# A third of a batch spread over two experts, small copies moved to ScalarE, and the first pair's sums moved into the third expert

## The chip, the core and the metric

The kernel runs on one NeuronCore of one Trainium2 chip. The metric is the device time of one execution in microseconds (us); lower is better. Shown are the median of 3 runs and one further execution that was profiled. The engines are TensorE (PE, with PEld for its weight loads), VectorE (DVE), ScalarE (ACT), GpSimd (POOL) and SyncE (SP), which here only issues DMAs.

## What is computed

Three stages follow one another. The input has 4 batches of 3072 rows of 256 values (12288 tokens).

```python
X = rfft(x, axis=1)                          # spectral layer, per batch
Yr = Xr @ w_r - Xi @ w_i + b_r ; Yi = Xr @ w_i + Xi @ w_r + b_i
Y = soft_threshold(Yr, 0.01) + 1j * soft_threshold(Yi, 0.01)
x = irfft(Y)                                 # rows go on as tokens
...
e = argmax(x @ w_gate)                       # 8 experts, 384 places each, first come first served
h = relu(disp @ w1[e]) ; y = h @ w2[e]       # 256 -> 1024 -> 256
out = gate * y                               # 0 for tokens without a place
...
h = out @ w_in ; g = h * sigmoid(h)          # 256 -> 2048 -> 256
return g @ w_out
```

An expert has 384 places, so no more than 3072 tokens get past the second stage. With this input the first batch and the first third (1024 rows) of the second fill all places, and the rest of the input is not transformed: that branch of the program (`far`, and `experts` with `again`) does not run.

## The kernel before, in words

Every matmul of the experts and of the last stage is done in three products (`mm3`, lines 206 to 210): each float32 operand is split into a rounded high part and a low remainder (`split`, lines 202 to 204: the high part by `hi`, L192, on ACT; the low part by `lo`, L200, on DVE or POOL), and PE multiplies high by high, low by high and high by low.

**Spectral part.** `near` transforms batch 0 and batch 1 up to about 190 us. The spectrum of batch 1, multiplied and thresholded, is stored by `kphase` to the DRAM tensor `b_d` (L497, on ACT's queue). What is left of batch 1, its last inverse step for the first 1024 rows, is `third` (lines 569 to 626). It has four pieces n = 0 to 3. For each, `rows(n)` fetches two blocks of 96 x 1024 values from `b_d` (384 KB each, L587, tile `br`, or `bi` and `by` where the block lies in memory lent by the tiles `ms` and `yT`), multiplies them (L590), copies the result out of PSUM (L595, ACT) and stores the tokens in four DMAs (L597). `gate(n)` transposes the tokens (L604), copies them out (L606, DVE, tile `aT`), multiplies by the gate's weights (L612), and for every second piece makes the choice of an expert (`choose`). Then `route` gives the 1024 tokens their places and `slots` makes the index lists of experts 3 to 7.

**Experts.** `experts` (lines 949 to 1038) goes through phases 0, 1, 2, E, 3, 4, E+1, 5, 6, E+2, 7, E+3: eight experts (`first_ffn`), and between them four parts of the last stage, each for a pair of experts (`second_ffn`). An expert's rows are gathered by indirect DMA (`gather`, L1084, tile `xg`), scaled by the gate (`turn`, L1095, DVE, three tiles of 128x256), transposed and split. Its loop has nine steps (lines 1113 to 1127): step j makes block j of the hidden layer (6 matmuls, tile `hp`), evicts it (L1120 ACT, L1121 DVE, tiles `hh` and `hl`) and adds block j-1 to the output (6 matmuls, tile `y`). The output has two halves, copied to `yf` (L1130 by ACT, L1131 by DVE). A counter n counts the steps over all phases: n = 1 to 9 is expert 0, 10 to 18 expert 1, 19 to 27 expert 2.

The weights of an expert come in four quarters of two loads of 256 KB (L1066, tile `st`, four buffers), each cast to a high part by ACT (L192, tile `w`) and completed by DVE or POOL. For experts 0 and 1 they are asked for one quarter at a time in the steps of expert 0 (`lazy`, line 1002). They are read from float32 arrays; the last stage's weights are 64-bit floats that DVE narrows (lines 880 to 901).

**Pairs.** `pair` (lines 1133 to 1164) turns the two outputs of a pair into the seven split operands of a product scheme with seven products in place of eight: four sums or differences by DVE (L1151, L1154, L1156, L1159), each split (tiles `yT` and `ms`). For the first pair it is called when phase E begins, and its first and last instruction are ordered behind `self.made`, the one-hot comparison of `route` (L756, tile `pm`).

**What sets the order.** A generator `beside` (lines 969 to 981) holds the rest of batch 1; `experts` advances it when the counter n reaches the value it last yielded. It yields 7, then 8, 10, 12, 14 and 16: `rows(0)` is written at n = 7, `rows(1)` and `gate(0)` at 8, `rows(2)` and `gate(1)` at 10, `rows(3)` and `gate(2)` at 12, `gate(3)` at 14, and `route`, `slots` and the rest at 16. The program is not run in the order in which it is written: the framework (`schedule_with_timeline_sim=True`) plays a timeline of its own and fixes each engine's order by it. `after(a, b)` tells it to put `a` behind `b` without a semaphore. In `rows` only the first matmul is put behind `self.lasty`, the newest `y` matmul; the fetches are not. Each engine and each DMA-issuing queue then runs its instructions strictly in that order.

Of the kernel before, what the change touches and what calls it, by code (L numbers as in the profile page):

```python
# [9 lines left out]
F32 = mybir.dt.float32  # L10
FR = mybir.dt.float32r
I32 = mybir.dt.int32
ALU = mybir.AluOpType
# [6 lines left out]
Q = 96  # L20
# [3 lines left out]
P = 128  # L24
# [16 lines left out]
RING = 2  # L41
LATE = 3
PACE = {4: 2, 5: 5, **{n: GT - 1 for n in range(6, 12)}}
HOLD = {10: "lt", 14: "bs", 18: "tb"}
BIG = 65536.0
UP = 65536.0
# [109 lines left out]
class Kernel:  # L156
# [412 lines left out]
    def third(self, b, res):  # L569

        nc, bp, ps, wg, CH = self.nc, self.bp, self.ps, self.wg, self.CH
        v = nc.vector
        c4 = self.c4[:Q, 64:]
        bv = self.bds[b].rearrange("k (r u g) c -> (k r) u (g c)", r=4, u=4)
        od = self.attn[0][b * S:b * S + QB * TW].rearrange("(q u g) d -> u q (g d)", u=4, g=GT)
        res[b] = self.chosen(1)
        idle = self.mg.tile([P, 3, 2, CH], F32, tag="ms", name="bi", bufs=1)
        room = {n + 2: idle[:Q, n] for n in range(3)}
        room[5] = self.mh.tile([P, 2, CH], F32, tag="yT", name="by", bufs=1)[:Q]

        def rows(n):
            pt = ps.tile([P, CH], F32, tag="ps", name="ps2")
            for w in range(2):
                br = room.get(2 * n + w)
                if br is None:
                    br = bp.tile([Q, 2, CH], F32, tag="xt", name="br", bufs=self.sb)
                nc.sync.dma_start(out=br, in_=bv[:, 2 * w:2 * w + 2, n * CH:(n + 1) * CH])  # L587
                for z in range(2):
                    u = 2 * w + z
                    ins = nc.tensor.matmul(pt[u * QB:(u + 1) * QB], c4, br[:, z], start=True, stop=True).ins  # L590
                    if b == 1 and not u:
                        self.after(ins, self.lasty)
            ao = bp.tile([P, 2, 2, P], F32, tag="ao", name="ao2")
            aof = ao.rearrange("p g h d -> p (g h d)")
            nc.scalar.copy(aof, pt)  # L595
            for u in range(4):
                nc.sync.dma_start(out=od[u, :, n * CH:(n + 1) * CH], in_=aof[u * QB:(u + 1) * QB])  # L597
            return ao

        def gate(n, ao):  # L600
            tp = ps.tile([P, 2, 2, P], F32, tag="ps", name="tp")
            for g in range(2):
                for h in range(2):
                    nc.tensor.transpose(tp[:, g, h], ao[:, g, h], self.ident)  # L604
            aT = bp.tile([P, 2, 2, P], F32, tag="aT", name="aT", bufs=1)
            v.tensor_copy(aT, tp)  # L606
            if n % 2 == 0:
                self.lg = ps.tile([P, P], F32, tag="ps", name="lg")
            for h in range(2):
                for g in range(2):  # L610
                    at = COL * (2 * (n % 2) + g)
                    nc.tensor.matmul(self.lg[at:at + COL], wg[:, h], aT[:, g, h], start=h == 0, stop=h == 1)  # L612
            if n % 2:
                ls = bp.tile([P, P], F32, tag="ls", name="ls", bufs=1)
                nc.scalar.copy(ls, self.lg)
                lt = ps.tile([P, 4, COL], F32, tag="ps", name="lt")
                nc.tensor.transpose(lt.rearrange("p g e -> p (g e)"), ls, self.ident)
                self.choose(lt.rearrange("p (o g) e -> p o g e", o=1)[:, :, :, :E], res[b], slice(2 * n - 2, 2 * n + 2))

        ao = {}  # L620
        for n in range(GT // 2 + 1):
            if n < GT // 2:
                ao[n] = rows(n)
            if n:
                gate(n - 1, ao.pop(n - 1))
            yield

    def is2(self, b, qbs, res):
# [320 lines left out]
    def experts(self, again=False):  # L949
        tc = self.tc  # L950
        tag = "b" if again else "a"
        st = self.ex

        def pool(name, bufs=1, **kw):
            return st.enter_context(tc.tile_pool(name=name + tag, bufs=bufs, reuse_waits="tile", **kw))

        right = dict(side="right")
        ps = dict(space=bass.MemoryType.PSUM)
        self.mq, self.mx, self.mh = pool("mq", 3, **right), pool("mx", 2, **right), pool("mh", 2, **right)
        self.ph, self.pm = pool("ph", 3, **right, **ps), pool("pm", 2, **right, **ps)  # L960
        self.again = again
        self.wo = pool("mo").tile([P, 2, DFF // P, D], FR, name="wo")
        self.mg, self.mc = pool("mg", 2), pool("mc")
        self.zr = self.mc.tile([P, 2 * D], FR, name="zr")

        def zeros():
            self.nc.gpsimd.tensor_copy(self.zr[:, D:], self.zt[:, 0])

        def beside():

            with self.stream("b", 2, "left"):
                yield 7
                for n, _ in enumerate(self.third(1, self.res)):
                    yield 8 + 2 * n
                tiny = self.mc.tile([P, 1], F32, name="tiny")
                self.route(1, (0,), self.res)
                self.sl.extend(self.slots(self.mc, EARLY, E, self.sel, "t")[0])
                self.after(self.nc.scalar.activation(tiny, self.zt[:, 0, :1], AF.Silu).ins, self.exps)
                self.filled()
                zeros()  # L980
            self.po, self.mb = pool("po", **ps), pool("mb")

        fw = self.ffn_out()
        if again:
            self.raws = self.out_rows()
            zeros()
            self.sl = self.compact(self.mc)
            self.po, self.mb = pool("po", **ps), pool("mb")
            side = iter(())
            for _ in self.ffn_in(0, 8):  # L990
                pass
        else:
            self.sl = list(self.early)
            side = beside()
        order = [0, 1, 2, E]
        for q in range(3, E, 2):
            order += [*range(q, min(q + 2, E)), E + q // 2]
        xs, self.ys, self.unit = {}, {}, {}
        xg = {e: self.gather(e) for e in order[:2]}
        xs[0] = self.turn(xg.pop(0))  # L1000
        ws = {e: self.weights(e, n) for e, n in zip(order[:2], (3, 4))}
        lazy = {0: (0, 1), 2: (0, 2), 3: (1, 0), 4: (0, 3), 5: (1, 1), 6: (1, 2), 7: (1, 3)}
        due = next(side, None)
        n = 0
        for at, ph in enumerate(order):
            if ph == E:
                for _ in side:
                    pass
                pre = self.pair(None if again else self.made)
            part = self.first_ffn(ph, xs.pop(ph), ws[ph][0]) if ph < E else self.second_ffn(ph - E, pre)  # L1010
            if ph >= E:
                next(part)
            after = order[at + 1] if at + 1 < len(order) else E
            if after < E and after not in ws:
                xg[after] = self.gather(after)
                ws[after] = self.weights(after, 4 if ph == E else 0)
            for m, _ in enumerate(part):
                n += 1
                if not at and m in lazy:
                    e, z = lazy[m]  # L1020
                    ws[e][1](z, self.rectified)
                while due is not None and due <= n:
                    due = next(side, None)
                if n in LOADS:
                    next(self.raws, None)
                if n in AHEAD or (ph == E and m < 2):
                    next(fw, None)
                if ph >= E:
                    if ph == E and 3 <= m < 7:
                        ws[after][1](m - 3, self.evicted)  # L1030
                    for _ in range(2):
                        self.zero_out()
                if m == 5:
                    behind = self.evicted
                if m == 6 and after < E:
                    xs[after] = self.turn(xg.pop(after), behind)
            if ph < E and ph > 1 and ph % 2:
                pre = self.pair()
# [53 lines left out]
    def turn(self, rows, behind=None):  # L1092
        xg, gw = rows
        for j in range(SC):
            ins = self.nc.vector.tensor_scalar(xg[:, j], xg[:, j], gw[:, j:j + 1], None, ALU.mult)  # L1095
            if behind:
                self.after(ins.ins, behind)
        xT = self.mx.tile([P, 2, 2, CAP], FR, tag="xT", name="xT")
# [7 lines left out]
    def first_ffn(self, e, xT, ws):  # L1106
# [21 lines left out]
            yield  # L1128
        y = self.ys[e] = self.mg.tile([P, 2, CAP], F32, tag="yf", name="yf", bufs=3)
        nc.scalar.copy(y[:, 0], yp[0])  # L1130
        nc.vector.tensor_copy(y[:, 1], yp[1])  # L1131

    def pair(self, behind=None):

# [256 lines left out]
```

## Time and profile before

| | |
|---|---|
| median of 3 runs | 616.54 us (615.39 to 617.16) |
| the profiled execution, its own time | 617.55 us |
| its span, from the first to the last instruction | 615.8 us |
| mean granted TensorE clock over the span | 0.988 |
| busy: PE / DVE / ACT / POOL | 593.4 / 424.7 / 339.3 / 187.0 us |

The span has three stretches: up to about 180 us the spectral part, from there to about 266 us the experts 0 to 2 with the rest of batch 1 and the start of phase E, and then the alternating phases up to 607 us, with the last scattered stores behind them. A row of the waits names the instruction that waited, what released it, the total, the count and the longest. A row of a timeline has the start, the duration, engine, line, operation, output and inputs, shape, count, and in brackets the idle time before it and its releaser. A clock of 1.00 is 2.4 GHz and 0.50 is 1.2 GHz.

### The profile page before, as it was taken

Reading aid. Unit: us, or ns where it says so; the run is one execution under the profiler, and the core shown is the slowest. Engines: PE = TensorE matmul, PEld = TensorE weight load, DVE = VectorE, ACT = ScalarE, POOL = GpSimd, SP = SyncE. Lnnn points to the kernel's source line nnn. Section 1 sums busy time; section 2 is a strip of 40 time slices with the busy share of each in tenths; the row PEclk is TensorE's granted clock in tenths of the full one; section 3 lists DMA queues with packets and bytes.
Section 4 is the critical chain, followed back from the end, with each engine's and each line's share of the span. In section 5 each row is a group of like instructions: output and inputs, shape, how many; then the busy total and the mean of one; then the engine's idle time right before and its main releaser. Section 6 shows DMA issues by size and latency. Waiting matters only on the chain. (4 is left out here: it accounts for less than half of the span.)

```text
span 615.8 us, 11426 instructions
## 1 busy us (share of the span) xinstructions
PE 593.4 (96%) x4104; PEld 556.1 (90%) x4104; DVE 424.7 (69%) x844; ACT 339.3 (55%) x723; POOL 187.0 (30%) x189
## 2 busy tenths in 40 slices
PE   9999999999989799899999999999999999999994
PEld 9887799667988589789999999999999999989994
DVE  2468765449977589998876786587587577486563
ACT  2546554336525465556765756655567556365562
POOL 1001110002053023177453505435403442154433
PEclk9999999999999799989999999999999999999998
DMA  8829775996357976433633532404433230010001
GB/s 223 254 78 277 249 219 168 250 278 180 105 183 209 248 226 191 143 120 99 197 120 116 169 125 97 155 23 138 150 113 106 91 100 26 0 65 27 16 2 56
DMA packets 65755, 86.09 MB, mean 140 GB/s; under 512 B 5812, under 2 KB 55608, under 8 KB 65688
## 3 DMA queue, kind: packets, MB, share of 16 engines
q1 hardware_dynamic: 53720, 69.53, 37.8%
q10 hardware_dynamic: 9664, 9.44, 5.2%
q0 software_dynamic: 2304, 6.29, 3.2%
q8 instruction: 34, 0.56, 0.4%
q14 instruction: 33, 0.27, 0.2%
HBM read 54.31 MB, written 30.93 MB: 138 GB/s over the span
## 5 line engine op out<-in xcount | busy, mean ns | idle before, releaser
L1289 DVE TENSOR_TENSOR u<-h,u 128x384 f32<-128x384 f32 x224 | 117.9, 552 | 59.9 <-PE h L210 51.6
L1199 ACT ACTIVATE u<-u 128x384 f32<-128x384 f32 x128 | 64.6, 522 | 73.1 <-DVE u L1289 71.1
L209 PE MATMUL o<-wo,gl 128*128 128x256 f32 x354 | 94.5, 280 | 0.9 <-DVE gl L200 0.9
L210 PE MATMUL o<-wo,gh 128*128 128x256 f32 x354 | 94.6, 280 | 0.0
L208 PE MATMUL o<-wo,gh 128*128 128x256 f32 x354 | 83.1, 280 | 0.0
L200 POOL TENSOR_TENSOR ring<-mt,ring 128x384 fp32r<-128x384 f32 x32 | 38.0, 1190 | 136.3 <-ACT ring L192 136.3
L200 POOL TENSOR_TENSOR gl<-u,gh 128x384 fp32r<-128x384 f32 x62 | 64.8, 1060 | 29.6 <-ACT gh L192 29.5
L209 PEld LDWEIGHTS o<-wo,gl 128*128 128x128 f32 x354 | 66.5, 188 | 1.2 <-DVE gl L200 1.2
L210 PEld LDWEIGHTS o<-wo,gh 128*128 128x128 f32 x354 | 66.5, 188 | 0.0
L192 ACT CAST gh<-u 128x384 fp32r<-128x384 f32 x126 | 63.1, 509 | 5.7 <-PE o L210 4.0
L208 PEld LDWEIGHTS o<-wo,gh 128*128 128x128 f32 x354 | 62.4, 188 | 0.0
L208 PE MATMUL yp<-wri,xk 128*128 128x256 f32 x188 | 56.1, 298 | 0.0
L210 PE MATMUL yp<-wri,xk 128*128 128x256 f32 x188 | 54.0, 287 | 0.0
L209 PE MATMUL yp<-wri,xk 128*128 128x256 f32 x188 | 53.7, 286 | 0.0
L192 ACT CAST w<-st 128x512 fp32r<-128x512 f32 x64 | 38.6, 619 | 23.5 <-DMA st<-in_moe_w 15.7
L200 DVE TENSOR_TENSOR w<-st,w 128x512 fp32r<-128x512 f32 x56 | 39.6, 717 | 17.1 <-ACT w L192 12.0
L1120 ACT ACTIVATE hh<-hp 128x384 fp32r<-128x384 f32 x64 | 31.1, 489 | 35.4 <-PE y L209 13.7
L1121 DVE SCALAR_TENSOR_TENSOR hl<-hp,hh 128x384 fp32r<-128x384 f32 x64 | 34.9, 552 | 21.6 <-ACT hh L1120 16.3
L200 POOL TENSOR_TENSOR wi<-na,wi 128x256 fp32r<-128x256 f32 (+1 forms) x8 | 8.1, 1012 | 132.9 <-ACT wi L192 132.9
L208 PE MATMUL hp<-xT,w 128*128 128x384 f32 x128 | 43.8, 343 | 4.2 <-ACT w L192 4.1
L200 DVE TENSOR_TENSOR gl<-u,gh 128x384 fp32r<-128x384 f32 x64 | 42.8, 669 | 2.2 <-ACT gh L192 2.1
L208 PE MATMUL y<-hh,w 128*128 128x384 f32 x128 | 43.7, 341 | 0.5 <-ACT hh L1120 0.5
(254 smaller groups left out, 1543.1 us busy)
## 6 DMA issues: line engine op xcount, KB each, us to landing
st<-in_moe_w SPq DMA_DIRECT2D x64, 256.0 KB, 2.9
out<-zt SPq DMA_DIRECT2D x48, 256.0 KB, 3.5
b_d<-bo ACTq DMA_DIRECT2D x12, 512.0 KB, 3.1
mt<-mixed SPq DMA_DIRECT2D x32, 192.0 KB, 2.3
xt<-in_x SPq DMA_DIRECT2D x15, 384.0 KB, 6.7
nt<-in_moe_w_in SPq DMA_DIRECT2D x8, 512.0 KB
nt<-in_moe_w_out SPq DMA_DIRECT2D x16, 256.0 KB, 3.0
a_d<-ao SPq DMA_DIRECT2D x8, 384.0 KB, 3.4
```

Source lines behind the costliest of these rows:

```text
L192: self.lastact = self.nc.scalar.copy(dst, src)
L200: return e.tensor_tensor(dst, src, raw(hi), ALU.subtract).ins
L208: first = nc.tensor.matmul(out, lh, rh, start=start, stop=False)
L209: nc.tensor.matmul(out, ll, rh, start=False, stop=False)
L210: return first.ins, nc.tensor.matmul(out, lh, rl, start=False, stop=stop).ins
L1120: self.rectified = nc.scalar.activation(hh, hp, AF.Relu).ins
L1121: self.evicted = nc.vector.scalar_tensor_tensor(hl, hp, 0.0, raw(hh), ALU.max, ALU.subtract).ins
L1199: act.activation(sg, sg, AF.Silu)
L1289: v.tensor_tensor(to, h, u, ALU.add)
```

## The change

`third` is cut into twelve steps instead of five. A step `f` fetches the two blocks of a piece, `r` multiplies and stores it, `g` does the gate. `STEPS` gives their order (f0 f1 r0 f2 g0 r1 f3 g1 r2 g2 r3 g3) and `DUE` the counter at which each is written: f0 at 5, f1 at 6, r0 at 7, f2 and g0 at 8, r1 at 9, f3 and g1 at 10, r2 at 11, g2 and r3 at 12, g3 and `route` with what follows it at 13. Every fetch is now put behind `self.lasty`, without a semaphore; the fetches of pieces 1 to 3 are issued on ACT's queue. Four copies `aT`, the 24 scalings `xg` and the eight copies of an output's second half go from DVE to ACT. `pair` for the first pair is called after the second step of expert 2 (n = 20), without the ordering behind `self.made`.

```diff
+STEPS = *zip("ffrfgrfgrgrg", (0, 1, 0, 2, 0, 1, 3, 1, 2, 2, 3, 3)),
+DUE = 5, 6, 7, 8, 8, 9, 10, 10, 11, 12, 12, 13, 13
...
-        def rows(n):
-            pt = ps.tile([P, CH], F32, tag="ps", name="ps2")
+        def fetch(n):
             for w in range(2):
                 br = room.get(2 * n + w)
                 if br is None:
-                    br = bp.tile([Q, 2, CH], F32, tag="xt", name="br", bufs=self.sb)
-                nc.sync.dma_start(out=br, in_=bv[:, 2 * w:2 * w + 2, n * CH:(n + 1) * CH])
-                for z in range(2):
-                    u = 2 * w + z
-                    ins = nc.tensor.matmul(pt[u * QB:(u + 1) * QB], c4, br[:, z], start=True, stop=True).ins
-                    if b == 1 and not u:
-                        self.after(ins, self.lasty)
+                    br = room[2 * n + w] = bp.tile([Q, 2, CH], F32, tag="xt", name="br", bufs=self.sb)
+                ins = (nc.scalar if n else nc.sync).dma_start(out=br, in_=bv[:, 2 * w:2 * w + 2, n * CH:(n + 1) * CH])
+                self.after(ins.ins, self.lasty)
+
+        def rows(n):
+            pt = ps.tile([P, CH], F32, tag="ps", name="ps2")
+            for u in range(4):
+                ins = nc.tensor.matmul(pt[u * QB:(u + 1) * QB], c4, room[2 * n + u // 2][:, u % 2], start=True, stop=True).ins
+                if not u:
+                    self.after(ins, self.lasty)
...
-            v.tensor_copy(aT, tp)
+            nc.scalar.copy(aT, tp)
...
-        for n in range(GT // 2 + 1):
-            if n < GT // 2:
+        for kind, n in STEPS:
+            if kind == "f":
+                fetch(n)
+            elif kind == "r":
                 ao[n] = rows(n)
-            if n:
-                gate(n - 1, ao.pop(n - 1))
+            else:
+                gate(n, ao.pop(n))
             yield
...
-                yield 7
+                yield DUE[0]
                 for n, _ in enumerate(self.third(1, self.res)):
-                    yield 8 + 2 * n
+                    yield DUE[n + 1]
...
-                pre = self.pair(None if again else self.made)
...
+                if m == 1 and at == 2:
+                    pre = self.pair()
...
-            ins = self.nc.vector.tensor_scalar(xg[:, j], xg[:, j], gw[:, j:j + 1], None, ALU.mult)
+            ins = self.nc.scalar.activation(xg[:, j], xg[:, j], AF.Copy, scale=gw[:, j:j + 1])
...
-        nc.vector.tensor_copy(y[:, 1], yp[1])
+        nc.scalar.copy(y[:, 1], yp[1])
```

## Rows read from the trace of the kernel before

**Rows 1.** The page, busy time, share of the span and instructions of each engine.
```profile
PE 593.4 (96%) x4104; PEld 556.1 (90%) x4104; DVE 424.7 (69%) x844; ACT 339.3 (55%) x723; POOL 187.0 (30%) x189
```
**Rows 2.** Waits of PE over the whole span: us in total, times, longest.
```profile
PE hp L208 <- ACT w L192: 4.1, 1, 4.1
PE h L208 <- ACT ms L192: 1.2, 1, 1.2
...
PE h L210 <- DVE ms L200: 1.2, 1, 1.2
...
PE gtp L1102 <- DVE xg L1095: 0.9, 1, 0.9
PE o L209 <- DVE gl L200: 0.9, 1, 0.9
```
**Rows 3.** Windows: length, busy of PE, PEld, DVE, ACT, POOL (count), PEclk, DMA share, GB/s.
```profile
195.00:210.00 15.00, 10.31 (x47) 7.56 (x46) 8.67 (x16) 6.18 (x13) 1.72 (x1) 0.82 1.05 240
...
204.50:211.33 6.83, 6.72 (x25) 4.62 (x26) 3.01 (x5) 3.00 (x7) 0.00 (x0) 0.50 1.08 256
...
255.00:262.53 7.53, 5.16 (x31) 4.53 (x30) 7.50 (x20) 4.13 (x9) 0.88 (x1) 1.00 0.05 15
262.53:265.94 3.41, 3.41 (x13) 3.37 (x11) 2.66 (x10) 0.68 (x1) 3.10 (x3) 0.50 0.25 74
...
275.00:600.00 325.00, 323.89 (x2208) 322.31 (x2207) 227.70 (x419) 198.64 (x426) 130.26 (x121) 1.00 0.29 92
```
**Rows 4.** Timeline of PE, in expert 0.
```profile
204.61 0.69 PE L208 MATMUL hp<-xT,w 128*128 128x384 f32 x1 [4.11 <-ACT w L192]
...
211.50 0.33 PE L208 MATMUL hp<-xT,w 128*128 128x384 f32 x1
211.67 0.34 PE L209 MATMUL hp<-xT,w 128*128 128x384 f32 x1
```
**Rows 5.** Timeline of ACT, the cast for which PE waited.
```profile
203.94 0.62 ACT L192 CAST w<-st 128x512 fp32r<-128x512 f32 x1 [5.88 <-DMA st<-in_moe_w]
```
**Rows 6.** Timeline of SP's queue, the issues from 194 to 199 us.
```profile
194.18 0.84 SPq L587 DMA_DIRECT2D br<-b_d  x2
195.12 0.39 SPq L587 DMA_DIRECT2D bi<-b_d  x1
195.76 1.00 SPq L1066 DMA_DIRECT2D st<-in_moe_w  x2
196.80 1.00 SPq L587 DMA_DIRECT2D bi<-b_d  x2
197.85 0.78 SPq L587 DMA_DIRECT2D by<-b_d  x1
```
**Rows 7.** Tiles `st`, then `br`, from 170 to 270 us: issue to landing.
```profile
DMA to landing us min/median/max: 2.7/3.0/8.2
...
DMA to landing us min/median/max: 7.2/7.2/7.2
```
**Rows 8.** Timelines of DVE, PE and POOL, around the start of phase E.
```profile
255.89 1.22 DVE L756 TENSOR_TENSOR pm<-iota,r 128x1024 fp32r<-128x1024 f32 x1
257.03 0.55 DVE L1151 TENSOR_TENSOR tm<-yf 128x384 f32<-128x384 f32 x1
...
260.40 0.44 PE L208 MATMUL h<-ms,wi 128*128 128x384 f32 x1 [1.22 <-ACT ms L192]
...
262.17 0.45 PE L210 MATMUL h<-ms,wi 128*128 128x384 f32 x1 [1.15 <-DVE ms L200]
...
261.65 3.20 POOL L200 TENSOR_TENSOR ring<-mt,ring 128x384 fp32r<-128x384 f32 x2 [10.61 <-ACT ring L192]
```
**Rows 9.** Lines 1095, 1130 and 1131: duration ns min/median/max, first and last start.
```profile
L1095 DVE TENSOR_SCALAR xg<-xg,gws x9: 338/341/1198, 180.0 to 232.5; 128x256 f32<-128x256 f32 x9
...
L1130 ACT COPY yf<-y x8: 461/474/479, 217.6 to 538.7; 128x384 f32<-128x384 f32 x8
...
L1131 DVE COPY yf<-y x8: 547/556/559, 217.8 to 538.6; 128x384 f32<-128x384 f32 x8
```

## The prediction

> **What bounds the kernel now.** The busy times come first: PE is busy for 593.4 us, 96% of the span, and no other engine is near that [rows 1]. No edit adds or removes a matmul, so the change can only win back time in which PE stands or runs slowly. Where that is, the waits of PE say [rows 2]: one of 4.1 us in expert 0, two of 1.2 us at the start of phase E, one of 0.9 us for the scaled rows `xg` and one of 0.9 us much later. The windows put these in their places [rows 3]. From 275 to 600 us PE is busy 323.89 of 325 us at full clock: nothing is to be won there, only lost. What can move lies between 180 and 266 us.
>
> The first hole: PE resumes at 204.61 after 4.11 us, and ACT's cast of a weight quarter ended the wait [rows 4]. ACT itself had waited for the load until 203.94 [rows 5]. SP's queue shows why the load was late: the pair of weight loads issued from 195.76 stands behind three fetches of the third, and three more follow by 197.85 [rows 6]. Six fetches of 384 KB are 2.36 MB, which at the 240 GB/s of this stretch is 9.8 us of all DMA engines, whose share reads 1.05, so they are full [rows 3]. A weight load elsewhere in this part lands in 3.0 us; the slowest took 8.2 us, and that is the one issued at 195.76 [rows 7] (195.76 + 8.2 = 203.96). When PE resumed, its granted clock was 0.50 for 6.83 us, the 1.2 GHz level [rows 3]; half of that, 3.4 us, is lost as well.
>
> The second hole: from 255 to 262.53 us PE is busy 5.16 of 7.53 us while DVE is busy for all of it [rows 3]. PE waits 1.22 and 1.15 us for the split sums `ms`, and DVE began them at 257.03, right after the one-hot `pm` of 1.22 us [rows 8], behind which the code pins them. After that the clock is at 0.50 for 3.41 us [rows 3], another 1.7 us.
>
> **The change, part by part.** *Fetches spread (steps f).* Eight fetches stay eight; none is added. f0 is put behind the `y` matmuls of its step, so the loads that were late, asked for in the same step just before it, go out ahead of it. Landing in 3.0 to 3.1 us from 195.76 and with a cast of 0.62 us [rows 5, 7] they would be ready at about 199.5, before the 200.5 at which PE stopped (204.61 - 4.11). So the 4.11 us and the 3.41 us at half clock should go: -7.52.
>
> What is late next is the fetch itself. A step is 12 matmuls of 0.17 us (211.50 to 211.67 [rows 4]), 2.0 us, and r0 comes two steps after f0, 4.1 us. From below, r0 waits 0. From above, a fetch lands in 7.2 us as the only one timed did [rows 7]: 3.1 us, plus up to 3.4 us of half clock. Between: two fetches are 0.79 MB, 3.3 us at 240 GB/s; a load's 2.7 us at best less the 1.1 us of its own bytes leaves 1.6 us; together 4.9 us, a wait of 0.8 us. With the two weight loads (0.52 MB, 2.2 us) still ahead it is 3.0 us. I take the middle, +2.0, and no half clock with it, as the clock still read 1.00 behind the first of the two waits of 1.2 us [rows 3, 8]. f1, f2 and f3 have three, three and two steps, the last with the work of r2 and g1 between: I take 0.
>
> *Six fetches on ACT's queue.* SP issues cost 0.39 to 0.78 us each [rows 6]; at that price ACT spends 2.3 to 4.7 us on six, over some ten. It is busy 6.18 of 15 us there [rows 3], which covers this. f1 and f2 go to lent tiles that nobody reads yet and wait for nothing; f3 reuses the buffers that r0 has read three steps before. Without that cover, the casts and evictions queued behind a waiting f3 come late, and PE for them. On SP the queue gets shorter, which can only help the weight loads.
>
> *`pair` in expert 2, `route` three steps earlier.* The first pair's operands come from experts 0 and 1, which come before expert 2, so its DVE and ACT work fits beside expert 2, and the pin behind `pm` is gone. The two waits (2.37 us by the window) and the 1.7 us of half clock should go: -4.07. What is late next: the ring of mixed weights, whose low halves POOL finishes 3.20 us after 261.65 [rows 8]. Its bounds are 0 (it starts earlier too) and the 2.4 us won; I take +0.5, nearer to 0, as nothing but its place in the order held it back.
>
> *Scaling and copies on ACT.* 24 scalings leave DVE, at 0.34 us and up to 1.2 us [rows 9]; on ACT they are bounded by the copy of a wider tile, 0.47 us. Four copies `aT` cost at most 0.62 us there, by the cast of that size [rows 5]. The second half of `yf` took DVE 0.56 us beside ACT's 0.47 [rows 9]; now ACT does both in turn and the pair is complete some 0.4 us later. The cover: `turn` is a step and more ahead of its use, and the first products of a pair need only the first expert's output. If it were gone, four pairs lose 4 x 0.47 = 1.9 us. I take 0, and 0 for DVE's relief, as PE's waits for DVE outside the pair are 0.9 us each [rows 2].
>
> **Sum.** On the profiled execution's own time: 617.55 - 7.52 - 4.07 + 2.0 + 0.5 = 608.46. That execution lies 1.01 above the median of the runs, so on the median: 607.45, rounded to 607.5. The best end is without the two additions and without the 0.93 us for `xg`: 616.54 - 11.59 - 0.93 = 604.0.
>
> **Rivals.** *Full DMA engines.* The bytes are the same, the stretch is full [rows 3], and PE now reaches expert 1 earlier; the hole only moves to expert 1's weights. Then 4.1 + 3.4 us stay and only the pair's part is won: 616.54 - 4.07 + 0.5 = 613.0. Against it: the jam is six fetches long, and now f1 and f2 come one and three steps behind f0 instead of with it. The Trainium skill, "DMA: Bandwidth & Descriptors", section "Issuing engines are not separate DMA queues", speaks for this rival: transfers issued by different engines interleave on the same 16 DMA engines, and a second issuer saves only issue time. By that page the move to ACT's queue wins nothing and only the later place of the fetches can, which is what the sum counts; if that fails too, 613.0 is its time.
>
> *The order is not what is written.* `after` is no wait, the framework's timeline may still place the fetches early and the sums late. Then nothing moves: 616.5, give or take 1.9.
>
> *Every piece waits for its own fetch (slower).* If a fetch beside weight loads takes the 7.2 us of [rows 7], the gaps of two, three, three and two steps (4.1, 6.1, 6.1, 4.1 us) leave waits of 3.1, 1.1, 1.1 and 3.1 us, 8.4 in all, and the two long ones bring 3.4 us of half clock each: 15.2 lost for 11.6 won, 616.54 + 3.6 = 620.1. It decides once a landing passes its gap by about 2.5 us. For it speaks the one row; against it, that this fetch went out into the jam the change takes away.
>
> **How the numbers follow.** The sum gets 0.60, with a range of its own from 604.0 to 610.5 (r0's wait doubled, and one copy exposed). The full engines get 0.17, the unmoved order 0.09, the waiting pieces 0.14. About 0.3% is what a measurement of this kernel can tell from no change, 1.9 us: below 614.7 is faster. Faster is 0.60 + 0.17 = 0.77, same 0.09, slower 0.14. The range 604.0 to 616.0 takes in the first two cases and a part of the third.
>
> **What would show it.** Right: the wait of `hp` for `w` under 1 us, no weight landing over 5 us in experts 0 and 1, fetches alternating with weight loads, clock 1.00 from 195 to 270 us, `ms` done before PE's first product of phase E, and 275 to 600 as dense as before. Wrong: PE waiting more than 2 us for a fetch ahead of the third's matmuls, a second half-clock stretch, evictions behind ACT's DMA issues, or a new wait for `ms` or `yf` at the later pairs.

## The result, and the profile after

The changed kernel takes 623.15 us (median of 8 runs, 620.78 to 625.24), the kernel before 616.85 us beside it (8 runs). The ratio is 1.0097, 95% interval 1.0078 to 1.0116: slower by 1%, where 607.5 us was forecast and the range ended at 616.0. The profiled execution after has a span of 621.4 us at a mean granted clock of 0.989; the one before has 615.8.

The waits of PE over the whole span, after:

```profile
PE y L210 <- issue: 2.8, 1, 2.8
PE y L210 <- ACT hh L1127: 2.2, 1, 2.2
PE y L212 <- DVE hl L1128: 1.4, 3, 0.6
...
PE hp L211 <- DVE w L202: 0.6, 2, 0.4
```

The wait of 4.1 us for a weight and the two of 1.2 us for `ms` [rows 2] are gone. In their place stand 2.2 us for an eviction `hh` and 2.8 us that end in no event the profile can name ("issue"). Windows of after (columns as in [rows 3], whose stretches the first four repeat) place them:

```profile
195.00:210.00 15.00, 13.97 (x77) 10.99 (x76) 12.22 (x21) 10.24 (x22) 3.00 (x2) 1.00 0.88 238
204.50:211.33 6.83, 6.51 (x39) 4.86 (x36) 3.83 (x8) 3.55 (x8) 1.28 (x1) 1.00 1.08 273
...
255.00:262.53 7.53, 6.54 (x40) 5.90 (x39) 5.52 (x23) 2.76 (x6) 0.41 (x1) 1.00 0.03 10
275.00:600.00 325.00, 321.52 (x2167) 318.79 (x2166) 210.63 (x393) 203.18 (x440) 125.95 (x119) 0.99 0.29 92
349.00:360.00 11.00, 8.08 (x29) 7.48 (x30) 6.96 (x15) 6.58 (x15) 2.59 (x3) 0.69 0.34 97
```

The two long waits of before are gone and the clock reads 1.00 from 195 to 262 us, as forecast. The loss is in the part called dense: in 11 us from 349 PE stands 2.92 us and runs at a mean clock of 0.69, which is 3.4 us more (11 x 0.31). Before, the same window is full:

```profile
349.00:360.00 11.00, 11.00 (x64) 10.77 (x63) 9.59 (x19) 6.29 (x15) 0.15 (x1) 1.00 0.46 146
```

To see where a lead is won and lost, count the 64 evictions `hh` of ACT (eight per expert, same order in every kernel) and take when the n-th ends, less the same in before. The 7th lies behind the first hole, the 11th early in expert 1, the 23rd at the end of expert 2, the 25th behind the first pair, the 39th at the end of expert 4. In us, minus is ahead; in brackets, when before ends that eviction:

| kernel | 7th (211.5) | 11th (223.8) | 23rd (253.9) | 25th (325.1) | 39th (358.3) | median us |
|---|---|---|---|---|---|---|
| after | -5.2 | 0.0 | 0.5 | 0.0 | 6.5 | 623.15 |
| e1 yf on DVE | -7.4 | -3.3 | 0.3 | 0.2 | 6.0 | 625.27 |
| e2 xg on DVE | -6.2 | 0.2 | 5.3 | 5.5 | 5.9 | 621.59 |
| e3 both on DVE | -6.1 | -0.5 | 1.3 | 1.3 | 1.3 | 619.00 |
| e4 six stores out | -5.8 | -0.9 | -0.4 | -0.9 | -0.1 | 617.32 |
| e5 third only | -6.3 | -0.6 | 1.4 | 4.6 | 4.6 | 619.81 |
| e6 pair only | -1.5 | -0.4 | 2.1 | 2.8 | 2.8 | 619.71 |
| e7 e3, f3 left out | -7.8 | -6.0 | -1.0 | -2.4 | -2.4 | 615.51 |
| e8 e3, lows on POOL | -7.9 | -2.4 | 2.8 | 2.6 | 2.6 | 622.40 |
| e9 before, xg on ACT | -5.0 | 0.7 | -0.3 | 0.5 | 6.4 | 622.66 |
| e13 e3, lows left out | -9.0 | -2.1 | -2.4 | -2.6 | -2.7 | 614.99 |
| e14 after, xg early | -8.1 | -2.2 | -0.7 | -0.8 | -0.4 | 617.54 |
| e15 e3, fetches earlier | -1.3 | 0.1 | 2.6 | 4.1 | 4.1 | 621.96 |
| e18 before, one part later | -1.9 | -2.1 | -2.3 | -1.7 | -2.0 | 614.51 |

After has two stories: a lead of 5 us at the 7th eviction that is gone by the 11th, and 6.5 us lost between the 25th and the 39th. At the first eviction, ahead of the third's fetches, the traces already lie between 1.4 us ahead (e17) and 1.8 us behind (after), so a difference of that size says little. Executions of one kernel lie several us apart (after 620.78 to 625.24, e17 616.30 to 624.39), and a trace is one of them (e8's took 618.21 us, e5's 621.96). So medians carry the verdicts and the traces the mechanisms.

**The lead lost by 224 us.** PE's waits there are 0.63 us at 217.80 for the copy `yf` and 2.19 us at 223.84 for an eviction `hh`, both on ACT. ACT itself stands 3.31 us in front of the first and 1.35 us for a weight load in front of the second (timeline of ACT, after):

```profile
214.60 1.67 ACTq L588 DMA_DIRECT2D br<-b_d  x2
216.37 0.62 ACT L194 CAST w<-st 128x512 fp32r<-128x512 f32 x1 [3.31 <-DMA nt<-in_moe_w_out]
```

The first line is f3, issued by ACT's own queue. The semaphores in the trace show that its two issues waited until f2's two blocks had landed, issued at 207.65 and 207.99 and landed at 214.52 and 215.92; all of ACT's later work stood behind them. (The bracket names another load, which landed just then.)

**The stall at 350 us.** POOL's timeline after, then before:

```profile
340.74 1.03 POOL L1344 DMA_INDIRECT out<-tail,dsts  x1 [10.39 <-ACT tail L1247]
342.07 1.00 POOL L1344 DMA_INDIRECT out<-tail,dsts  x1 [0.30 <-issue]
...
348.53 1.04 POOL L1091 DMA_INDIRECT xg<-attn,srct  x1 [0.30 <-issue]
349.88 1.01 POOL L1091 DMA_INDIRECT xg<-attn,srct  x1 [0.31 <-issue]
351.19 1.00 POOL L1091 DMA_INDIRECT xg<-attn,srct  x1 [0.30 <-issue]
```

```profile
333.15 1.02 POOL L1337 DMA_INDIRECT out<-tail,dsts  x1 [3.79 <-ACT tail L1240]
334.48 1.00 POOL L1337 DMA_INDIRECT out<-tail,dsts  x1 [0.30 <-issue]
339.52 1.34 POOL L1337 DMA_INDIRECT out<-tail,dsts  x1 [4.04 <-ACT tail L1240]
...
345.49 1.04 POOL L1084 DMA_INDIRECT xg<-attn,srct  x1 [0.31 <-PE hp L210]
```

The same nine indirect DMAs (six stores of the tail, three gathers) run in one piece after and in pieces of two and seven before; "in one piece" means that no more than 0.31 us lies between two. What moved them is ACT's written order: the copies of `o` to the tail, which release the stores, stand behind the new scalings; the first of these copies starts at 339.89 us, in before at 332.29 (timeline of ACT, after):

```profile
338.68 1.31 ACT L1102 ACTIVATE xg<-xg,gwt 128x256 f32<-128x256 f32 x3
339.89 1.06 ACT L1247 COPY tail<-o 128x512 f32<-128x512 f32 x2
...
352.32 0.49 ACT L1127 ACTIVATE hh<-hp 128x384 fp32r<-128x384 f32 x1 [2.22 <-remote]
352.71 0.47 ACT L1137 COPY yf<-y 128x384 f32<-128x384 f32 x1
```

And PE (timeline, after):

```profile
347.34 0.51 PE L212 MATMUL y<-hl,w 128*128 128x384 f32 x2
...
353.24 0.69 PE L210 MATMUL y<-hh,w 128*128 128x384 f32 x1 [2.77 <-issue]
```

Expert 3's last `y` product ends at 347.85. Its copy `yf`, which frees the PSUM buffer for expert 4's `y`, starts at 352.71, behind an `hh` that had waited for PE's signal until 352.3, 0.1 us after POOL's last gather (351.19 + 1.00). PE resumes when the copy ends, at the lower clock.

### The profile page after: what moved, and what is told of

Its sections match the earlier page's. It is cut to its first block, busy times and chain, and to the rows that moved or that the text cites. A ratio compares the mean times of both kernels' runs of the same rounds, so it can differ in the third digit from the quotient of the medians.

```text
span 621.4 us, 11436 instructions
## 1 busy us (share of the span) xinstructions
PE 596.9 (96%) x4104; PEld 556.0 (89%) x4104; DVE 405.1 (65%) x808; ACT 353.5 (57%) x759; POOL 183.5 (30%) x189
## 5 line engine op out<-in xcount | busy, mean ns | idle before, releaser
L210 PE MATMUL hp<-xT,w 128*128 128x384 f32 x128 | 44.8, 351 | 0.9 <-DVE xT L202 0.6
L211 PE MATMUL hp<-xT,w 128*128 128x384 f32 x128 | 43.8, 342 | 0.6 <-DVE w L202 0.6
```

The costliest lines, as they stand in the source:

```text
L210: first = nc.tensor.matmul(out, lh, rh, start=start, stop=False)
L211: nc.tensor.matmul(out, ll, rh, start=False, stop=False)
```

## The experiments

Two theories for the stall came first: A, the second `yf` copy in turn on ACT, behind work that waits for PE; B, the nine DMAs in a row. C is both together.

**e1, e2, e3: parts put back on DVE.** e1 has the first edit, e2 the second, e3 both.

```diff
-        nc.scalar.copy(y[:, 1], yp[1])
+        nc.vector.tensor_copy(y[:, 1], yp[1])
...
-            ins = self.nc.scalar.activation(xg[:, j], xg[:, j], AF.Copy, scale=gw[:, j:j + 1])
+            ins = self.nc.vector.tensor_scalar(xg[:, j], xg[:, j], gw[:, j:j + 1], None, ALU.mult)
```

> The kernel after with one copy put back: the second half of yf on DVE (L1138). Measured so far: after 623.15, before 616.85; the loss lies at 349 to 360 us, where PE stands 2.77 us at 353.24 and then runs 6.83 us at a granted clock of 0.50. Theory A (the second copy in turn on ACT): in that stretch it sits behind a cast that waits for PE, which waits for the first copy; without it the stall and its half clock go, about 617 (6.2 us back). Theory B (nine indirect DMAs in a row on POOL, 340.7 to 352.2 us, and PE's completion signals that reach ACT only when that run ends): the run stays nine long, the signal for hh stays 5 us late, and the time stays at 623 (at most 0.5 us of copy back). Theory C (both are needed: a late signal does harm only with the serial copy behind it): about 617, with the signal still 5 us late.

> The kernel after with the 24 scalings of xg put back on DVE (L1102); both halves of yf stay on ACT. The written order of ACT then has the three tail copies of pair (0,1) apart from each other again, as in before. Theory A: the serial copy is still there, 623. Theory B: the six scatters go out in two groups as in before (2 and 4), no run of POOL is longer than seven indirect DMAs, and no signal is later than about 2 us; the stall at 353 us and its half clock go, about 617. Theory C: about 617 as well.

> Both put back on DVE, the second half of yf and the scalings of xg; the spread fetches, the early pair and the copies of aT on ACT stay. Theories A, B and C: no stall at 353 us, 617 or less. If the 3.5 us that were given back at 217 to 254 us were given back by ACT's added work (waits for yf and hh on ACT), then about 613; if by the spread fetches themselves, 617.

Measured: e1 625.27 us (ratio 1.0188, 1.0144 to 1.0231), e2 621.59 (1.0099, 1.0076 to 1.0123), e3 619.00 (1.0051, 1.0029 to 1.0074). Windows of e1, then two of e2:

```profile
349.00:360.00 11.00, 7.63 (x32) 6.80 (x32) 7.01 (x15) 6.94 (x14) 2.74 (x3) 0.84 0.36 103
```

```profile
235.00:255.00 20.00, 16.29 (x101) 14.16 (x100) 19.89 (x40) 13.04 (x28) 7.90 (x7) 0.96 0.75 245
349.00:360.00 11.00, 10.78 (x62) 10.25 (x61) 9.50 (x19) 8.44 (x18) 4.38 (x5) 1.00 0.60 178
```

A falls, and C with it: e1 has no serial copy and the full stall, e2 has the copy and no stall. For e2's time B was wrong all the same. It loses about 5 us earlier, between the 11th and the 23rd eviction, where DVE is busy 19.89 of 20 us and PE waits 3.31 us for a low half `hl` (252.65). In e3 neither stall is there, and still nothing is won.

**e4, e9, e14: the run of nine by itself.** e4 leaves the six stores out and keeps ACT's work and its order, e9 puts the scalings alone into the kernel before, e14 keeps them on ACT only ahead of phase E.

```diff
# e4
-            for e in range(2):
+            for e in range(2 if q > 1 or self.again else 0):
                 out(q - 1, s_, oo, e)
# e14, in turn
+        turned = self.turned = getattr(self, "turned", -1) + 1
...
+            if self.again or turned > 2:
+                ins = self.nc.vector.tensor_scalar(xg[:, j], xg[:, j], gw[:, j:j + 1], None, ALU.mult)
```

> The kernel after, leaving out the six indirect stores of the rows of pair (0,1) in its first pass (those of L1344 that follow its tail copies), so that their rows of the output are not written; the copies of the rows into the tail tile stay, as does every other instruction, in the same order. POOL's run of indirect DMAs at 341 us is then three long, not nine. Theory A: the serial copy is untouched, 623. Theory B: hh gets PE's signal within 1 us, the stall and its half clock at 353 us go, about 617. Theory C: about 617 too.

> The kernel before with one thing changed: the 24 scalings of xg on ACT. Its written order on ACT then has the three tail copies of pair (0,1) in a row right behind the scalings, as in the kernel after. Theory B: POOL issues nine indirect DMAs in a row near 340 us, PE's signals reach ACT late until the run ends, and PE stands about 2.8 us with half clock behind it near 350 us: 616 + 3 to 6 = 619 to 622. Rival: the run alone does nothing, the loss at 350 us needed the other parts of the change as well: 615 to 617.

> The kernel after with the scalings of xg on ACT for experts 0 to 2 alone and on DVE from expert 3 on; everything else of the change stays, the second half of yf on ACT too. Theory B: the tail copies of pair (0,1) are apart again, POOL's longest run there is seven, the stall at 350 us is gone: 617 to 619, 5 us under after. If the copy of yf on ACT costs by itself (theory A in a weaker form), 620 to 622 as the kernel with all scalings on DVE and yf on ACT.

Measured: e4 617.32 us (ratio 1.0016, 0.9997 to 1.0035), e9 622.66 (1.0105, 1.0074 to 1.0136), e14 617.54 (1.0024, 1.0001 to 1.0048). The window of e9, then of e14:

```profile
349.00:360.00 11.00, 7.40 (x32) 6.42 (x31) 7.02 (x14) 6.63 (x14) 3.06 (x3) 0.84 0.33 99
```

```profile
349.00:360.00 11.00, 10.78 (x61) 10.26 (x60) 8.77 (x18) 6.67 (x15) 0.00 (x0) 1.00 0.44 139
```

B holds: the stores, moved up against the gathers, make the stall. e9 has none of the spread, the pair or the copies and loses as much as the whole change; e14 has all of the change but 15 of the 24 scalings and gets 5.6 us back, the second `yf` copy still on ACT; e4 has ACT's new order without the stores, and no stall. The stores' bytes are no rival: the DMA engines are 0.34 busy in after's window. From the traces, the end of expert 3's last `y` product and the start of its first `yf` copy:

| kernel | indirect DMAs in one run | `y` ends | `yf` starts | POOL's run ends |
|---|---|---|---|---|
| before | 7 | 347.54 | 347.62 | 349.15 |
| e14 | 7 | 346.70 | 346.77 | 348.32 |
| e4 | 3 | 346.98 | 347.06 | 346.14 |
| after | 9 | 347.85 | 352.71 | 352.20 |
| e1 | 9 | 348.00 | 352.43 | 352.35 |
| e9 | 9 | 348.38 | 352.83 | 352.73 |

In e4 the run was over when the product ended; before and e14 show that a run of seven, still going, does no harm.

**e5, e6: the third alone, the pair alone.** e5 is before with the diff's `STEPS`, `DUE`, `fetch` (its six issues on ACT's queue with it) and `rows`; e6 is before with:

```diff
-                pre = self.pair(None if again else self.made)
...
+                if m == 1 and at == 2:
+                    pre = self.pair()
```

> Of the change only the spread third (its step table, the six fetches on ACT's queue); pair, scalings and copies as in before. Forecast's theory: 4.1 us of wait and 3.4 us of half clock go and a part stays gone, 616 - 7.5 + 2 = about 610. Theory D (the DMA engines are full from 200 to 220 us whatever the order of the transfers, so PE gains at 205 us and stands later for the loads behind the last fetches): the lead over before is 6 us or more at the seventh eviction of expert 0 (211 us), under 1 us at the third eviction of expert 1 (224 us), and the time is 614 to 617. If the lead lasts to 224 us and is lost between 230 and 255 us instead, theory E (DVE has no time left there) is the one.

> Of the change only the sums of the first pair moved into expert 2; all else as in before. Forecast's theory: the waits of 1.2 and 1.15 us and the half clock at 262.5 us go, 616 - 4.1 + 0.5 = about 612. Theory E (DVE is busy 4.7 to 4.9 of every 5 us from 230 to 245 us in before, so the sums only push the low halves hl and the gating of the third later): the waits of phase E go, new ones of the same size come ahead of it, 615 to 618, with the half clock gone or moved.

Measured: e5 619.81 us (ratio 1.0058, 1.0042 to 1.0074), e6 619.71 (1.0058, 1.0045 to 1.0071). Each is slower alone. e5's lead goes as theory D (full DMA engines) said, and it loses 3 us more behind expert 2, which its expected 614 to 617 us didn't foresee: PE waits 3.35 us there for DVE's one-hot `pm`. In e6, as theory E (no time left on DVE) said, PE waits for `hl` behind the sums (timeline of DVE, then of PE):

```profile
242.68 1.38 DVE L1152 TENSOR_TENSOR tm<-yf 128x384 f32<-128x384 f32 x1
...
247.56 1.42 DVE L200 TENSOR_TENSOR ms<-tm,ms 128x384 fp32r<-128x384 f32 x1
248.90 0.55 DVE L1122 SCALAR_TENSOR_TENSOR hl<-hp,hh 128x384 fp32r<-128x384 f32 x1
```

```profile
249.50 0.88 PE L210 MATMUL y<-hl,w 128*128 128x384 f32 x2 [2.27 <-DVE hl L1122]
```

**e7, e10, e15: the bytes.** All edit e3. e7 leaves f3 out (r3 computes from f2's tiles), e10 puts it behind r2, e15 asks for f0 to f2 three or four steps earlier on POOL's queue.

```diff
# e7
-STEPS = *zip("ffrfgrfgrgrg", (0, 1, 0, 2, 0, 1, 3, 1, 2, 2, 3, 3)),
+STEPS = *zip("ffrfgr-grgrg", (0, 1, 0, 2, 0, 1, 3, 1, 2, 2, 3, 3)),
# e10
+STEPS = *zip("ffrfgrgrfgrg", (0, 1, 0, 2, 0, 1, 1, 2, 3, 2, 3, 3)),
+DUE = 5, 6, 7, 8, 8, 9, 10, 11, 11, 12, 12, 13, 13
# e15
+STEPS = *zip("fffrgrfgrgrg", (0, 1, 2, 0, 0, 1, 3, 1, 2, 2, 3, 3)),
+DUE = 2, 3, 4, 7, 8, 9, 9, 10, 11, 12, 12, 13, 13
+                ins = (nc.scalar if n > 2 else nc.gpsimd).dma_start(out=br, ...
```

> The kernel with yf and xg on DVE (618 to 619 measured), leaving out the last two fetches of the third (0.79 MB): its last piece is computed from the tiles of the piece before, so those rows are not the reference's. Theory D: the nt load and the st load for which DVE and ACT stand until 220.25 and 222.19 us land about 3 us earlier, PE's wait of 2.46 us at 221 us is gone, the lead over before at 224 us is 3 us instead of 0.5; the time falls by up to 3 us, 615 to 616, or by less than 1 us if theory E takes the rest at 230 to 255 us. Forecast's theory, which counts no cost for these two: no change, 618 to 619.

> The kernel with yf and xg on DVE (619 measured), the last two fetches issued one step later, behind the third piece, so that the nt and st loads go out ahead of them; they are used at 230 us only. Theory D: the wait of 2.46 us for hl at 221 us goes, the lead over before at 224 us is 3 us; if it lasts, 616; if DVE takes it between 230 and 255 us (theory E), 618 to 619.

> The kernel with yf and xg on DVE (619 measured), the first three fetches asked for three steps earlier and on POOL's queue, so that they go out as soon as their source is written (about 193 us), where the DMA engines are 64% busy, and not from 195 us on, where they are full. Theory D: the same bytes are through earlier, so the loads behind them land 1 to 3 us earlier and the lead over before at 224 us is 1.5 to 3.5 us instead of 0.5; the time 616 to 618, or 619 if DVE takes the rest. If a lead at 224 us does not appear, the bytes are not what holds it.

Measured: e7 615.51 us (ratio 0.9989, 0.9976 to 1.0003), e10 619.57 (1.0045, 1.0027 to 1.0064), e15 621.96 (1.0091, 1.0061 to 1.0121). What e3 waits for near 221 us, in its timelines of DVE, ACT and PE, in turn:

```profile
220.32 0.43 DVE L904 TENSOR_SCALAR nsg<-nt 128x512 int32<-128x512 int32 x1 [2.36 <-DMA nt<-in_moe_w_out]
220.66 0.55 DVE L1128 SCALAR_TENSOR_TENSOR hl<-hp,hh 128x384 fp32r<-128x384 f32 x1
```

```profile
222.24 0.62 ACT L194 CAST w<-st 128x512 fp32r<-128x512 f32 x1 [1.24 <-DMA st<-in_moe_w]
```

```profile
221.27 0.62 PE L212 MATMUL y<-hl,w 128*128 128x384 f32 x2 [2.30 <-DVE hl L1128]
```

DVE and ACT work in order and both stand for a load, with PE's evictions behind. With 0.79 MB less (e7) the lead at the 11th eviction is 6.0 us instead of 0.5. e7 takes f3's wait off ACT's queue as well. e10 takes that wait away too (ACT issues f3 at 216.38, right behind a cast that stood until 216.24 for its own load) but keeps the bytes, and its lead at the 11th is 0.8, where 3 was expected. So it is the bytes that hold PE there, and another order of them doesn't help. In e15 four fetches go out ahead of a weight load issued at 195.93 and two right behind it, on another engine's queue, and the old hole is back (timeline of PE, then tile `st`):

```profile
210.22 0.69 PE L210 MATMUL y<-hh,w 128*128 128x384 f32 x1 [6.00 <-ACT hh L1127]
```

```profile
DMA to landing us min/median/max: 2.6/3.1/13.2
```

That load took 13.2 us, against 8.2 in before [rows 7]. The Trainium skill, "DMA: Bandwidth & Descriptors", section "Issuing engines are not separate DMA queues", says that DMAs of different issuing engines interleave on the same 16 DMA engines. This run agrees: fetches on POOL's queue held up a load on SP's. e15 missed its expectation for it: earlier fetches meant later weights.

**e8, e13, e16: DVE's work in the pair.** On e3, the five low halves of the first pair's `ms` move to POOL (e8) or are left out (e13); e16 is e13 and e15 together.

```diff
-            self.split("av", t[:, 0], t[:, 1], src)
+            self.split("ap" if e == 0 else "av", t[:, 0], t[:, 1], src)
```

> The kernel with yf and xg on DVE (618 to 619 measured), with the five low halves of ms of the first pair alone on POOL instead of DVE. Theory E: DVE is what holds 230 to 270 us; five instructions of about 0.55 us less there give back up to 2.7 us, 616 to 617, if POOL has them ready before phase E needs them at 260 us; if POOL is late, PE waits for ms there and nothing is won. Theory D alone: the stretch is held by the loads, and the time stays at 618 to 619.

> The kernel with yf and xg on DVE (619 measured), leaving out the five low halves of ms of the first pair (five DVE instructions of 0.55 us; PE's products use the high half twice, so the work of PE is unchanged). Theory E (DVE's time in 230 to 270 us holds PE): the wait of 1.18 us for hl at 249 us and those for u and ring behind it shrink, 1 to 2.7 us less, 616 to 618. If the stretch is held by loads or by the order alone: 619.

> Both of these together: fetches earlier on POOL's queue, and leaving out the five low halves of the first pair. Theories D and E together: each hides the other's gain when alone, so this one gains more than their sum, 613 to 615. If the two gains only add or less: 616 or more.

Measured: e8 622.40 us (ratio 1.0091, 1.0075 to 1.0107), e13 614.99 (0.9987, 0.9967 to 1.0008), e16 620.17 (1.0056, 1.0037 to 1.0076). 2.7 us of DVE work less give 4.0 us against e3 (619.00), and PE's wait of 1.02 us for `hl` in e3 (249.44) is gone: DVE holds this stretch. By the table, 2.2 of the 3.7 us between the two traces at the 23rd eviction arise behind the 11th, where the sums lie; the rest is there before them. e16 missed, as it carries e15's hole. On POOL the halves cost more than they save (e8, whose trace, its fastest execution, shows 1.3 us of the 3.4 that lie between it and e3; timelines of DVE, POOL and PE, in turn):

```profile
244.45 1.37 DVE L1163 TENSOR_TENSOR yf<-yf 128x384 f32<-128x384 f32 x1
```

```profile
242.65 1.46 POOL L202 TENSOR_TENSOR ms<-yf,ms 128x384 fp32r<-128x384 f32 x1
244.07 2.61 POOL L202 TENSOR_TENSOR ms<-tm,ms 128x384 fp32r<-128x384 f32 x2
```

```profile
250.43 1.01 PE L212 MATMUL y<-hl,w 128*128 128x384 f32 x2 [3.94 <-DVE hl L1128]
```

**e11, e12, e17, e18: towards a better version.** e11 is e10 with the early scalings of e14; e12 is e11 with the pair at `m == 3`; e17 is e14, and e18 is before, with

```diff
-AHEAD = 1, 4, 7, 12, 16, 20
+AHEAD = 1, 4, 7, 12, 16
...
-                if n in AHEAD or (ph == E and m < 2):
+                if n in AHEAD or (ph == E and m < 3):
```

> The kernel of the last fetches one step later, and besides the scalings of xg on ACT for experts 0 to 2 alone (all that come ahead of phase E), so that no tail copy is moved. Theory E: three instructions of 0.34 to 1.2 us less on DVE between 225 and 262 us are 1.7 us less in front of hl and the sums: 1 to 2 us under that kernel, about 615 to 617. If the time does not fall, DVE's total is not what holds this stretch but the order of its work.

> The kernel of the run before, with the sums of the first pair emitted two steps later in expert 2 (step 3, not 1). Theory E with the order as the cause: the evictions hl near 249 us go ahead of the sums, their wait of 1.2 to 2.4 us goes, and the sums are still there by 260 us: 614 to 616. If the sums are late, PE waits for ms at the start of phase E, as in before: 617 to 619.

> The kernel after with the scalings on ACT for experts 0 to 2 alone (617.5 measured), and one more part of the output weights (of eight, some 2.6 us of DVE: L900, L904 to L906, and its low half on POOL) left for phase E, so that expert 2 has one less. Theory E: DVE's time in 240 to 255 us holds PE, and 2.6 us less there give 1 to 3 us as the 2.7 us left out from ms did: 614.5 to 616.5, under both kernels. If phase E has no room on DVE at 270 to 280 us, or the loads behind 220 us hold it, 617 to 618.

> The kernel before with that one edit alone: one more part of the output weights left for phase E. Before, DVE works without a break from 250 to 265 us and PE waits twice for the sums there. Theory E: 1 to 2 us less, 614 to 615. If the sums hang on the order of the routing and its pin and not on DVE's time: 616, as before.

Measured: e11 620.68 us (ratio 1.0078, 1.0058 to 1.0097), e12 621.86 (1.0098, 1.0079 to 1.0116), e17 618.84 (1.0065, 1.0038 to 1.0092), e18 614.51 (0.9981, 0.9965 to 0.9996). The first three missed. e17's trace is 2.2 us ahead of before at the 23rd eviction and 0.1 behind at the 25th: the lead is lost in the first pair's phase. Of the kernels that leave no work out only e18 beats both, by 0.2% over before, and it uses nothing of the change.

## Why the prediction was wrong

The sum won 9.1 us (7.52 + 4.07 - 2.0 - 0.5) up to the first pair and lost nothing behind it. In the trace nothing is left of the gain at the 25th eviction (0.0, or the 1.8 us by which this trace started late), and 6.5 us are lost behind it.

*Fetches spread (-7.52 + 2.0).* The mechanism was right and its end was not. Wait and half clock at 204.6 us are gone, and the third's first products wait 0.44 us for a fetch instead of the 2.0 counted. But the sum treated the gain as kept. The stretch holds the same bytes through full DMA engines, and PE gives the lead back at 217 to 224 us, behind the `nt` and `st` loads. This was the first rival (613.0 us, chance 0.17): it named the cause and put the new hole in the right expert. In e5 the third alone is 3.5 us slower than before (619.81 to 616.27), not 5.5 faster.

*Pair in expert 2 (-4.07 + 0.5).* Wrong by its cover, "DVE and ACT work fits beside expert 2". The waits for `ms` went, as said, but the sums pushed `hl` back, and alone they cost 3.4 us (e6). The prediction read DVE as full in the window from 255 us alone [rows 3]; in the 20 us ahead of it, where the sums were to go, before has DVE busy 18.38 us:

```profile
235.00:255.00 20.00, 19.47 (x121) 18.56 (x118) 18.38 (x46) 10.35 (x22) 6.68 (x7) 1.00 0.67 214
```

The sums' price was short as well: two of e6's take 1.38 and 1.42 us instead of 0.55, beside instructions of POOL at 242.35 and 247.18. And phase E got other waits for the two that went: 0.39 us for `yf`, 0.60 for the ring (0.5 was counted), 0.78 for `u` and 1.15 for `gl`, 2.92 us for 2.37. Only the half clock there was won.

*Scalings on ACT (0).* The step that cost the most. Their own time was small, as bounded: 1.31 us for three. The sum asked only what the instruction costs where it lands, not what stands behind it: the tail copies were placed after the scalings, the stores after the copies, and 6.5 us went at 350 us, in a stretch where "nothing is to be won, only lost". e9 shows the scalings alone doing it, e14 their absence undoing it.

*Second `yf` copy on ACT (0, at most 1.9).* Not shown to cost anything by itself: e14 keeps it and is at 617.54. e2 against e3 (621.59 to 619.00) differ in it alone, so it can cost where DVE is full; by which path wasn't isolated.

*Six fetches on ACT's queue (0).* The cover was wrong: that ACT is busy 6.18 of 15 us says nothing of what stands behind an issue that waits. f3 waited not for r0's buffers but for f2 to land, and ACT stood 3.3 us with it, the case that the prediction names as the end of its cover. PE's own wait behind it is 0.63 us, and in e10, without it, the lead is gone all the same, so it decided nothing here. The four `aT` copies were not tried apart.

*The slower rival* (each piece waits for its own fetch, 620.1 us, 0.14) came near the time by the wrong cause. Fetches did take 7 us to land (f2's 6.9 and 7.9), but in after no wait of PE ahead of the third's products passes 0.5 us.

*Signs named.* Of the signs for right, clock and `ms` came as written, and no weight landing over 5 us did not: the load issued at 199.97 took 7.5 us, the one at 216.02 took 6.7. Of those for wrong, two came: evictions behind ACT's DMA issues (213 to 216 us), and a half-clock stretch, at 353 us and not where the gain was looked for.

## What to carry to other kernels

Price a moved instruction by what is queued behind it on its new engine, down to the DMAs that this releases, and a DMA issue by the work that stands behind it while it waits; follow that chain into the stretches called dense. When a wait is removed, ask which resource is full from there to the next hole: here DMA up to 224 us and DVE from 230 to 270 us, so closing a hole only moved it. A gain is counted when it is still there a stage later, and counting the same instruction in both traces shows at once where it goes.

## What the hardware showed

While POOL issued nine indirect DMAs in a row, 1.3 us each, PE's finished products reached ACT 4.4 us late or more, and each time within 0.2 us of the end of the run (after 352.20 to 352.32, e1 352.35 to 352.43, e9 352.73 to 352.83). It builds up: the eviction before, at 348.01 in after, had already waited 2.58 us for PE. In before and e14, in the middle of a run of seven, the same signal took 0.08 us. So it isn't the issuing alone. Nor is it the length alone, or six stores alone: in e7 and e15 nine gathers run unbroken from 174 to 187 us and no wait of PE there passes 0.81 us, and in after six stores run unbroken from 548 to 556 us and none passes 0.35. What it is in six stores with three gathers behind them that holds the signal back stays open.

In e8 DVE's instructions on SBUF operands take 1.37 us instead of the 0.55 that they take in e3 (245.55) while POOL runs one of its own (above), and `hl`, which reads PSUM, stays at 0.55. From 243.16 to 249.84 five such instructions take 7.06 us, 4.3 us more than the same five in e3, where 2.7 us were taken off DVE. The Trainium skill, "SBUF — State Buffer", section "Who interferes with whom", says that DVE and GpSimd share one pair of ports under an exclusive lock. The trace agrees, and it is how work taken off DVE and given to POOL made e8 slower than e3, by 3.4 us in the medians. It isn't always DVE that pays: in before two `ms` halves take 1.02 us together at 261.56 beside POOL's `ring` [rows 8].
